# Moving w2 and the last part of wo behind the last value head, two sums behind two value heads, and the result's turn to VectorE

## The chip, the cores and the metric

The kernel runs on one core of one Trainium2 chip. The metric is the device time of one execution in microseconds. The kernel before takes 200.01 us, the median of three runs (199.66 to 200.16).

## What is computed

One decoding step of a gated mix of two branches. Branch A is attention of a single token over a cache of 4,096 positions with 32 heads of 128, followed by an output projection. Branch B is a small MLP with a squared ReLU. The gate is one scalar.

```python
x = A_x                                                     # 1 x 1 x 512
g = sigmoid((x * gate_w).sum(-1))
q = (x @ wq)                                                # 512 -> 32 heads x 128
p = softmax(einsum("bhqd,bhkd->bhqk", q, k) * 128**-0.5)    # 4096 positions
a = einsum("bhqk,bhkd->bhqd", p, v).reshape(1, 1, 4096) @ wo    # 4096 -> 512
h = relu(x @ w1 + b1)                                       # 512 -> 1376
b = (h * h) @ w2 + b2                                       # 1376 -> 512
return g * a + (1 - g) * b
```

All inputs and the result are bf16. Each key head and each value head is 1,024 KB, so 64 loads of that size are most of what is moved; wq and wo are 4,096 KB each, w1 and w2 1,376 KB each.

## The kernel before, in words

**Staging.** Eight key slots (`Kt`) and eight value slots (`Vt`), each 128 x 4,096 bf16, are refilled as their heads are used up. The SP queue issues nearly all loads in one written-out order: wq, seven key heads, then for every `h` the value head `h` and the key head `h + LAG` with `LAG = 7`. `load_k` waits until VectorE (`s_sd`) and TensorE (`s_t`) are through with the slot's former head, `load_v` until the PV product of the slot's former head (`s_pv`). Between these loads SP issues the four parts of w1 at `h == 8`, the first eight column groups of w2 (`w2a[:, 0:8, :]`, 1,024 KB) at `h == 10`, and five strips of wo at `h` 20 to 24. The other strips of wo's first 23 heads go over GpSimd's queue into `W`, where wq had been. Behind value head 31 SP issues four small or mid-sized pieces into key slots and w2 tiles: `wox` (the rows of wo for head 23, 128 KB), `w2b` (the last 96 rows of w2, 96 KB), `w2a[:, 8:10, :]` (256 KB) and `wob_sb` (the rows of wo for heads 24 to 31) in two parts of 768 and 256 KB.

**Scores.** Of each key head, VectorE multiplies and sums half of the blocks (`ttr`, L635), and TensorE turns the other half (`transposes`, L432), which ScalarE copies out and TensorE multiplies by the query (`scores`, L443). VectorE joins the halves (`smax`, L641). A maximum over four heads is made through `max_rows`, `gmax` and `max_cols`, and ScalarE takes the exponentials.

**The main loop** counts `i` from 0 to 38 on every engine. On TensorE, round `i` turns key head `i`, scores head `i - 1` and makes the PV product of head `i - 7` (`pv`, L468: 32 matmuls with one column each). MLP work is put in at `i == 24` (`mlp_h`) and `i == 27` (`mlp_out(0)`: 32 matmuls with `w2a[:, 0:8, :]`, L553). From `i == 34` on, `out_a` multiplies the parts of the projection that TensorE does for the first 23 heads' spread result (L512), while VectorE sums the other nine column groups by itself (`part_y`, L682 and L685, into `yD`). `sum_y(0)` and `sum_y(1)` (L544, four fp32 matmuls each in the trace) add that sum over the partitions into the accumulator `acc`; in rounds 36 and 37 they stand ahead of `pv(29)` and `pv(30)`. All partial results of the output, of both branches, go into `acc` in PSUM.

**The tail**, behind `pv(31)`: `norm(3)` on VectorE (L662), then `regroup` on TensorE: a transpose (L518), four matmuls with `wox` (L521), four with `w2b`, and, after VectorE's copy `oB` (L718), 16 matmuls that spread the eight heads (L526). Then `mlp_out(2)` (eight matmuls with `w2a[:, 8:10, :]`), VectorE's copy `o2B` (L720), and `out_b` (32 matmuls with `wob_sb`, L535). VectorE adds the bias (`fin`, L723), TensorE turns the 128 x 4 result to 4 x 128 (L598), VectorE copies it out of PSUM (`fin4`, L725), and SP stores it as four pieces of 256 B (L298).

[...] The functions that the change touches, and what calls them:

Of the kernel before, what the change touches and what calls it, by code (L numbers as in the profile page):

```python
# [5 lines left out]
def bass_gated_mix__gqa_block_cached__dense_activation_squared_relu__decode_kernel(  # L6
# [22 lines left out]
    bf16 = mybir.dt.bfloat16  # L29
    ALU = mybir.AluOpType  # L30
# [23 lines left out]
    NA = 24  # L54
    TB = 8
    GS = [0, 8, 10]
    TS = [0, 6, 8]
    TD = 23
    INNER, OUTER, SEAM, WRAP = range(4)
    RUNS = [(INNER, 4, 12, 0, 2), (INNER, 4, 12, 1, 2),  # L60
# [43 lines left out]
    with ctx:  # L104
        def sb(name, shape, dt):
            return ctx.enter_context(nc.sbuf_tensor(name, shape, dt))
# [28 lines left out]
        oB = sb("oB", [NH - NA, 128], bf16)  # L135
        o2A = sb("o2A", [128, 32], bf16)
        o2B = sb("o2B", [128, TB], bf16)
        fin4 = sb("fin4", [4, 128], bf16)
        zeros = sb("zeros", [128, 128], bf16)
        xb = sb("xb", [128, 4, 128], bf16)  # L140
        dm = xb[:, :, :].rearrange("p t (n a c) -> p (t n) a c", a=2, c=16)
# [18 lines left out]
        hr = sb("hr", [128, FG + 1], fp32)  # L160
        hs = sb("hs", [128, FG + 1], bf16)
        b2g = sb("b2g", [128, 4], fp32)
        fin = sb("fin", [128, 4], bf16)

        KP = [pb(f"KP{i}", [128, HB * 128], bf16) for i in range(3)]
        pS = pb("pS", [128, 512], fp32)
# [30 lines left out]
        s_wq = [sem(f"s_wq{t}") for t in range(4)]  # L197
        s_w1 = sem("s_w1")
        s_w2 = [sem(f"s_w2{n}") for n in range(len(GS))]
        s_wo = [sem(f"s_wo{n}") for n in range(len(TS) - 1)]  # L200
        s_wp = [sem(f"s_wp{n}") for n in range(len(RUNS))]
        s_dm = [sem(f"s_dm{n}") for n in range(len(RUNS))]
        s_at = sem("s_at")
# [3 lines left out]
        s_oT = sem("s_oT")  # L207
        s_oc = sem("s_oc")
        s_o2 = sem("s_o2")
        s_fT = sem("s_fT")  # L210
        s_f4 = sem("s_f4")
        s_k = [sem(f"s_k{i}") for i in range(NK)]
        s_v = [sem(f"s_v{i}") for i in range(NV)]
# [39 lines left out]
        @block.sync  # L253
        def _(eng):
            for t in range(4):
                eng.dma_start(wq_sb[:, t, :], wq_v[:, t, :]).then_inc(s_wq[t], 16)  # L256

            def load_k(h):
                if h >= NK:
                    eng.wait_ge(s_sd, h - NK + 1)  # L260
                    eng.wait_ge(s_t, 2 * (h - NK + 1))
                eng.dma_start(Kt[:, h % NK, :], k_h[h, :, :]).then_inc(s_k[h % NK], 16)

            def load_v(h):
                if h >= NV:
                    eng.wait_ge(s_pv, h - NV + 1)
                eng.dma_start(Vt[:, h % NV, :], v_h[h, :, :]).then_inc(s_v[h % NV], 16)

            for h in range(LAG):
                load_k(h)  # L270
            for h in range(NH):
                load_v(h)
                if h + LAG < NH:
                    load_k(h + LAG)
                if h == HF:
                    eng.wait_ge(s_qps, 8)
                if HF <= h < HF + len(FIRST):
                    p, st, k, q = STRIPS[len(RUNS) + h - HF]
                    eng.dma_start(W[p:p + st * (k - 1) + 1:st, :], woa_v[q:q + k, :],
                                  max_dma_last_dim=8192).then_inc(s_wr, 16)  # L280
                if h == 8:
                    eng.wait_ge(s_z, 1)
                    eng.wait_ge(s_b2, 1)
                    for t in range(4):
                        eng.dma_start(w1_sb[:, t, :], w1_v[:, t, :]).then_inc(s_w1, 16)
                if h == 10:
                    eng.dma_start(w2a[:, 0:GS[1], :], w2_v[:, 0:GS[1], :]).then_inc(s_w2[0], 16)
            eng.wait_ge(s_sd, NA + 2)
            eng.wait_ge(s_t, 2 * (NA + 2))
            eng.dma_start(wox, A_wo[HX * 128:NA * 128, :]).then_inc(s_wx, 16)  # L290
            eng.dma_start(w2b[:, :], B_w2[FG * 128:F, :]).then_inc(s_w2[1], 16)
            eng.dma_start(w2a[:, GS[1]:FG, :], w2_v[:, GS[1]:FG, :]).then_inc(s_w2[2], 16)
            for c in range(len(TS) - 1):
                eng.dma_start(wob_sb[:, TS[c]:TS[c + 1], :],
                              wob_v[:, TS[c] * DM:TS[c + 1] * DM].rearrange("p (t n) -> p t n", n=DM))\
                   .then_inc(s_wo[c], 16)
            eng.wait_ge(s_f4, 1)
            eng.dma_start(out[0, 0, :].rearrange("(j p) -> j p", p=128), fin4[:, :]).then_inc(s_out, 16)  # L298
            eng.wait_ge(s_out, 16)


# [90 lines left out]
        def _(eng):  # L392
# [111 lines left out]
            def out_a(n):  # L504
                if n == 0:
                    eng.wait_ge(s_ac, 2)
                    for q in s_wp:
                        eng.wait_ge(q, 16)
                    eng.wait_ge(s_wr, 16 * len(FIRST))
                for t in range(4 * n, min(4 * n + 4, TD)):  # L510
                    for j in range(4):
                        eng.matmul(acc[:, j:j + 1], wo_sb[:, t, j * 128:(j + 1) * 128],  # L512
                                   o2A[:, t:t + 1], start=False, stop=False,
                                   skip_group_check=True)

            def regroup():
                eng.wait_ge(s_on, NH // HPO)
                eng.transpose(KP[0][0:NH - NA, 0:128], onorm[:, NA:NH], ident[:, :]).then_inc(s_oT, 1)  # L518
                eng.wait_ge(s_wx, 16)
                for j in range(4):  # L520
                    eng.matmul(acc[:, j:j + 1], wox[:, j * 128:(j + 1) * 128], onorm[:, HX:HX + 1],  # L521
                               start=False, stop=False, skip_group_check=True)
                mlp_out(1)
                eng.wait_ge(s_oc, 1)
                for c in range(16):
                    mm = eng.matmul(O2B, selB[:, c // 8, c % 8, :], oB[:, TB * c:TB * c + TB],  # L526
                                    start=(c == 0), stop=(c == 15))
                mm.then_inc(s_oT, 1)

            def out_b(c):  # L530
                eng.wait_ge(s_o2, 1)
                eng.wait_ge(s_wo[c], 16)
                for t in range(TS[c], TS[c + 1]):
                    for j in range(4):
                        mm = eng.matmul(acc[:, j:j + 1], wob_sb[:, t, j * 128:(j + 1) * 128],  # L535
                                        o2B[:, t:t + 1], start=False, stop=(t == TB - 1),
                                        skip_group_check=True)
                if c == len(TS) - 2:
                    mm.then_inc(s_acc, 1)

            def sum_y(c):
                eng.wait_ge(s_y, 32 - TD)
# [4 lines left out]
            def mlp_out(c):  # L547
                eng.wait_ge(s_w2[c], 16)
                for n in [range(GS[1]), [FG], range(GS[1], FG)][c]:
                    M = 128 if n < FG else FR  # L550
                    w = w2a[:, n, :] if n < FG else w2b[:, :]
                    for j in range(4):
                        eng.matmul(acc[:, j:j + 1], w[:, j * 128:(j + 1) * 128], hs[0:M, n:n + 1],  # L553
                                   start=(n == 0 and j == 0), stop=False, skip_group_check=True)

            q_rows(0)
            q_cols(0)
# [3 lines left out]
            for i in range(NH + LAG):  # L561
                if i < NH:
                    transposes(i)
                if 1 <= i <= NH:
                    scores(i - 1)
                if i % 3 == 0 and i // 3 + 1 < 8:
                    q_rows(i // 3 + 1)
                if i % 3 == 2 and i // 3 + 1 < 8:
                    q_cols(i // 3 + 1)
                if i >= 5 and (i - 5) % 4 == 0 and (i - 5) // 4 < NG:  # L570
                    max_rows((i - 5) // 4)
                if i >= 6 and (i - 6) % 4 == 0 and (i - 6) // 4 < NG:
                    max_cols((i - 6) // 4)
                if i == 34:
                    out_a(0)
                if 34 <= i < 39:
                    out_a(i - 33)
                if 36 <= i < 38:
                    sum_y(i - 36)
                if i >= LAG:  # L580
                    pv(i - LAG)
                if i >= 12 and (i - 12) % HPO == 0:
                    den((i - 12) // HPO)
                if i == 24:
                    mlp_h()
                if i == 27:
                    eng.wait_ge(s_hs, 2)
                    mlp_out(0)
                if i == 32:
                    turn_a()  # L590
                if i == 33:
                    spread_a()
            regroup()
            mlp_out(2)
            for c in range(len(TS) - 1):
                out_b(c)
            eng.wait_ge(s_fin, 1)
            eng.transpose(KP[1][0:4, 0:128], fin[:, :], ident[:, :]).then_inc(s_fT, 1)  # L598


        @block.vector
        def _(eng):
            eng.memset(zeros[:, :], 0.0).then_inc(s_dz, 1)
            eng.wait_ge(s_dz, 1)
            eng.wait_ge(s_x, 32)
            eng.tensor_tensor_reduce(grow, xrow, grow, 1.0, 0.0, ALU.mult,
# [113 lines left out]
            eng.tensor_copy(o2B[:, :], O2B).then_inc(s_o2, 1)  # L720
            eng.wait_ge(s_acc, 1)
            eng.wait_ge(s_g, 4)
            eng.tensor_tensor(fin[:, :], acc[:, 0:4], b2g[:, :], ALU.add).then_inc(s_fin, 1)  # L723
            eng.wait_ge(s_fT, 1)
            eng.tensor_copy(fin4[:, :], KP[1][0:4, 0:128]).then_inc(s_f4, 1)  # L725


# [26 lines left out]
```

## Time and profile before

| | |
|---|---|
| median of three runs | 200.01 us |
| profiled execution, its own time | 199.44 us |
| its span, first to last instruction | 197.6 us |
| busy: TensorE matmul / weight load | 67% / 60% |
| busy: VectorE / ScalarE / GpSimd | 70% / 40% / 15% |
| DMA: moved, mean rate over the span | 78.76 MB, 398 GB/s |
| the loads' queue (SP), share of 16 DMA engines | 93.1% |
| TensorE's mean granted clock | 0.589 |

Times are microseconds from the span's start unless marked ns. In a timeline row the columns are start, length, engine, line, operation, out<-in, count, and in brackets the engine's idle time before it with what ended it. "issue" there means that the engine waited for nothing that the profile shows. In a row of a DMA view the last number is the median time in us from issue to landing. PE is TensorE's matmul, PEld its weight load, DVE VectorE, ACT ScalarE, POOL GpSimd, and SPq the issuing queue of SP.

### The profile page before, as it was taken

How to read it: one execution, taken by the hardware profiler on the slowest of the kernel's cores; microseconds unless marked ns; L12 is line 12 of the kernel's file. 1: busy time of each engine (PE TensorE's matmuls, PEld its weight loads, DVE VectorE, ACT ScalarE, POOL GpSimd, SP SyncE). 2: the span in 40 equal slices, each digit the busy share in tenths (PEclk: the TensorE clock that was granted, in tenths of full speed). 3: DMA queues.
4: the chain of work that ended last, by engine and by line, in shares of the span. 5: the costliest groups of instructions: out<-in, count | busy, mean ns of one | idle time of the engine just before them, and what ended most of it. 6: DMA issues, size and time to landing. Idle time of an engine off the chain costs nothing.

```text
span 197.6 us, 6567 instructions
## 1 busy us (share of the span) xinstructions
PE 132.4 (67%) x2403; PEld 119.0 (60%) x2409; DVE 139.0 (70%) x1151; ACT 79.6 (40%) x148; POOL 30.0 (15%) x53
## 2 busy tenths in 40 slices
PE   0138856799886757816567572766999876797465
PEld 0105845678686557616457462766998776787464
DVE  0307999999998687627665774767759999968501
ACT  2105857366473436503337232633048333613000
POOL 2000000000000000000008970000079770000000
PEclk9999985555555855555558555555555555555555
DMA  6999999999999999999999999999999999999970
GB/s 226 425 426 424 421 418 424 416 421 418 413 418 419 416 422 409 419 418 424 421 419 420 411 416 410 415 406 415 410 416 416 423 418 416 421 419 419 393 270 6
DMA packets 12861, 78.76 MB, mean 398 GB/s; under 512 B 2505, under 2 KB 2731, under 8 KB 3628
## 3 DMA queue, kind: packets, MB, share of 16 engines
q1 hardware_dynamic: 11278, 75.77, 93.1%
q0 software_dynamic: 1536, 2.56, 3.5%
q8 instruction: 19, 0.31, 0.6%
q14 instruction: 14, 0.11, 0.2%
q10 hardware_dynamic: 14, 0.01, 0.0%
HBM read 78.32 MB, written 0.00 MB: 396 GB/s over the span
## 4 chain that ended last, share of the span: by engine, by line
DMA 64%; DVE 23%; PE 9%; issue 2%; SPq 1%; ACT 0%; DVEq 0%
DMA Kt<-in_A_k_cache_dram 58%; DVE Kt L635 17%; DMA W<-in_A_wq_dram 6%; DVE kT L685 3%; PE pQ L468 2%; DVE S L635 1%; PE KP L432 1%; PE pQ L410 1%; PE pX L544 1%; SPq L256 1%; PE pS L443 1%; PE pX L535 0%; PE pO L468 0%; PE pX L512 0%; DVE S L641 0%
## 5 line engine op out<-in xcount | busy, mean ns | idle before, releaser
L635 DVE CUSTOM_DVE_ANT_0 Kt<-Kt,qb 128x128 bf16<-128x128 bf16 x512 | 113.3, 290 | 26.1 <-DMA Kt<-in_A_k_cache_dram 26.0
L366 ACT ACTIVATE kT<-KP 128x1024 bf16<-128x1024 bf16 x64 | 61.9, 1021 | 72.4 <-PE KP L432 72.4
L432 PE MATMUL KP<-ident,Kt 128*128 128x128 bf16 x512 | 57.5, 302 | 36.1 <-DMA Kt<-in_A_k_cache_dram 36.1
L432 PEld LDWEIGHTS KP<-ident,Kt 128*128 128x128 bf16 x512 | 49.8, 140 | 38.6 <-DMA Kt<-in_A_k_cache_dram 37.7
L635 DVE DVE_READ_ACCUMULATOR2_ANT S<- 128x1 f32 x512 | 41.6, 81 | 0.0
L443 PEld LDWEIGHTS pS<-qcol,kT 128*128 128x128 bf16 x512 | 18.7, 108 | 9.5 <-DVE S L641 9.4
L443 PE MATMUL pS<-qcol,kT 128*128 128x1 bf16 x512 | 19.2, 167 | 7.2 <-DVE S L641 7.2
L320 POOL DMA_DIRECT2D xb<-in_B_w_dram x9 | 5.3, 593 | 102.5 <-PE pQ L410 102.5
L410 PE MATMUL pQ<-W,xb 128*128 128x512 bf16 x26 | 11.4, 576 | 7.5 <-DMA W<-in_A_wq_dram 6.2
L468 PE MATMUL pO<-E,Vt 128*128 128x1 bf16 x512 | 16.1, 165 | 0.0
L468 PEld LDWEIGHTS pO<-E,Vt 128*128 128x128 bf16 x512 | 15.4, 104 | 0.9 <-issue 0.5
L338 POOL TENSOR_SCALAR_AFFINE_SELECT w_sb<-w_sb 24x36 bf16<-24x36 bf16 (+5 forms) x19 | 11.0, 579 | 2.7
L358 ACT ACTIVATE qb<-pQ 128x512 bf16<-128x512 f32 x8 | 4.7, 592 | 13.9 <-PE pQ L410 13.9
L377 ACT ACTIVATE E<-S,nM 128x32 bf16<-128x32 f32 x32 | 9.9, 309 | 0.3
L410 PEld LDWEIGHTS pQ<-W,xb 128*128 128x128 bf16 x32 | 3.5, 126 | 10.4 <-issue 10.1
L468 PE MATMUL pQ<-E,Vt 128*128 128x1 bf16 x256 | 8.1, 165 | 1.7 <-issue 1.2
L468 PEld LDWEIGHTS pQ<-E,Vt 128*128 128x128 bf16 x256 | 7.9, 106 | 1.9 <-issue 1.8
L468 PEld LDWEIGHTS pX<-E,Vt 128*128 128x128 bf16 x256 | 7.8, 104 | 0.7 <-issue 0.6
L468 PE MATMUL pX<-E,Vt 128*128 128x1 bf16 x256 | 8.1, 165 | 0.0
L323 POOL DMA_DIRECT2D W<-in_A_wo_dram x14 | 7.9, 565 | 0.0
L641 DVE COPY S<-pS 128x16 f32<-128x16 f32 x32 | 5.4, 169 | 2.3 <-PE pS L443 2.3
L621 DVE CAST qcol<-pQ 128x4 bf16<-128x4 f32 x8 | 1.2, 153 | 8.3 <-PE pQ L418 8.3
(85 smaller groups left out, 91.5 us busy)
## 6 DMA issues: line engine op xcount, KB each, us to landing
Kt<-in_A_k_cache_dram SPq DMA_DIRECT2D x32, 1024.0 KB, 27.4
Vt<-in_A_v_cache_dram SPq DMA_DIRECT2D x32, 1024.0 KB, 27.1
W<-in_A_wq_dram SPq DMA_DIRECT2D x4, 1024.0 KB, 7.9
W<-in_A_wo_dram POOLq DMA_DIRECT2D x2, 768.0 KB, 12.8
w_sb<-in_B_w_dram SPq DMA_DIRECT2D x4, 344.0 KB, 22.9
w2a<-in_B_w_dram SPq DMA_DIRECT2D x1, 1024.0 KB, 21.5
Kt<-in_A_wo_dram SPq DMA_DIRECT2D x1, 768.0 KB, 21.3
W<-in_A_wo_dram POOLq DMA_DIRECT2D x10, 64.0 KB, 23.3
```

What stands on the lines that cost most here:

```text
L320: eng.dma_start(dm[0:d, sent, :, 0:8], src[:, :, 0:8]).then_inc(s_dm[sent], 16)
L323: eng.dma_start(W[p:p + st * (k - 1) + 1:st, :], woa_v[q:q + k, :], max_dma_last_dim=8192).then_inc(s_wp[n], 16)
L338: eng.affine_select(out=part, in_=part, compare_op=ALU.not_equal, fill=1.0, base=-st * q, pattern=[[st, 4], [-1, st * (k - 1) + 1]], chann ...
L366: eng.activation(kT[:, h % 2, j * HB * 128:(j + 1) * HB * 128], KP[n % 3][:, :], ACT.Copy).then_inc(s_ev, 1)
L377: eng.activation(E[:, h % NE, :], S[:, h % NS, :], ACT.Exp, bias=nM[:, h:h + 1], scale=SCALE, accum_out=RS[:, h:h + 1]).then_inc(s_e, 1)
L410: mm = eng.matmul(pQ[:, :], xb[:, t, :], wq_sb[:, t, c * 512:(c + 1) * 512], start=(t == 0), stop=(t == 3))
L432: mm = eng.transpose(KP[n % 3][:, y * 128:(y + 1) * 128], Kt[:, h % NK, b * 128:(b + 1) * 128], ident[:, :])
L443: mm = eng.matmul(S2[:, y:y + 1], kT[:, h % 2, y * 128:(y + 1) * 128], qcol[:, h:h + 1], start=True, stop=True)
L468: mm = eng.matmul(O(h, h + 1), Vt[:, h % NV, b * 128:(b + 1) * 128], E[:, h % NE, b:b + 1], start=(b == 0), stop=(b == NB - 1))
L635: ins = eng.tensor_tensor_reduce(kb, kb, qb[:, h * 128:(h + 1) * 128], 1.0, 0.0, ALU.mult, ALU.add, S[:, h % NS, b:b + 1])
L641: eng.tensor_copy(S[:, h % NS, XB:NB], S2).then_inc(s_cp, 1)
L685: eng.scalar_tensor_tensor(out=yD, in0=wo_sb[:, t, :], scalar=o2D[:, t - TD:t - TD + 1], in1=yD, op0=ALU.mult, op1=ALU.add).then_inc(s_y, 1)
```

## The change

- `w2a[:, 0:8, :]` is no longer issued at `h == 10`; it stands behind value head 31. The order there is now `wob_sb` as one transfer of 1,024 KB, `w2a[:, 0:8, :]`, `wox`, `w2b`, `w2a[:, 8:10, :]`.
- On TensorE all of `mlp_out` moves to the very end, and the matmuls with `wox` leave `regroup`: behind `regroup` come `out_b`, `mlp_out(0)`, `out_x`, `mlp_out(1)`, `mlp_out(2)`. The accumulation's start flag goes to the first matmul of `out_a`, its stop flag and the semaphore `s_acc` to `mlp_out(2)`.
- In rounds 36 and 37 `pv` now stands ahead of `sum_y`.
- The result is turned on VectorE: `fin` becomes 128 x 4 x 32, cleared at the start, and the result goes into column 0 of each block of 32; a block transpose of 128 x 128 (in 32 x 32 blocks) brings it into rows 0, 32, 64 and 96 of `finT`. The TensorE transpose and the copy out of PSUM are gone. SP stores 16 pieces of 64 B.

```diff
# sync
-                if h == 10:
-                    eng.dma_start(w2a[:, 0:GS[1], :], w2_v[:, 0:GS[1], :]).then_inc(s_w2[0], 16)
             eng.wait_ge(s_sd, NA + 2)
             eng.wait_ge(s_t, 2 * (NA + 2))
+            eng.dma_start(wob_sb[:, :, :], wob_v.rearrange("p (t n) -> p t n", n=DM)).then_inc(s_wo, 16)
+            eng.dma_start(w2a[:, 0:GS[1], :], w2_v[:, 0:GS[1], :]).then_inc(s_w2[0], 16)
             eng.dma_start(wox, A_wo[HX * 128:NA * 128, :]).then_inc(s_wx, 16)
             eng.dma_start(w2b[:, :], B_w2[FG * 128:F, :]).then_inc(s_w2[1], 16)
             eng.dma_start(w2a[:, GS[1]:FG, :], w2_v[:, GS[1]:FG, :]).then_inc(s_w2[2], 16)
-            for c in range(len(TS) - 1):
-                eng.dma_start(wob_sb[:, TS[c]:TS[c + 1], :], ...).then_inc(s_wo[c], 16)
             eng.wait_ge(s_f4, 1)
-            eng.dma_start(out[0, 0, :].rearrange("(j p) -> j p", p=128), fin4[:, :]).then_inc(s_out, 16)
+            eng.dma_start(out[0, 0, :].rearrange("(j k a) -> k j a", j=4, k=4),
+                          finT[0:97:32, :].rearrange("k (j a) -> k j a", j=4)).then_inc(s_out, 16)
# tensor
-                if 36 <= i < 38:
-                    sum_y(i - 36)
                 if i >= LAG:
                     pv(i - LAG)
+                if 36 <= i < 38:
+                    sum_y(i - 36)
...
-                if i == 27:
-                    eng.wait_ge(s_hs, 2)
-                    mlp_out(0)
...
             regroup()
+            out_b()
+            eng.wait_ge(s_hs, 2)
+            mlp_out(0)
+            out_x()
+            mlp_out(1)
             mlp_out(2)
-            for c in range(len(TS) - 1):
-                out_b(c)
-            eng.wait_ge(s_fin, 1)
-            eng.transpose(KP[1][0:4, 0:128], fin[:, :], ident[:, :]).then_inc(s_fT, 1)
# vector
             eng.memset(zeros[:, :], 0.0).then_inc(s_dz, 1)
+            eng.memset(fin[:, :, :], 0.0).then_inc(s_fin, 1)
...
-            eng.tensor_tensor(fin[:, :], acc[:, 0:4], b2g[:, :], ALU.add).then_inc(s_fin, 1)
-            eng.wait_ge(s_fT, 1)
-            eng.tensor_copy(fin4[:, :], KP[1][0:4, 0:128]).then_inc(s_f4, 1)
+            eng.tensor_tensor(fin[:, :, 0], acc[:, 0:4], b2g[:, :], ALU.add).then_inc(s_fin, 1)
+            eng.wait_ge(s_fin, 2)
+            eng.transpose(finT[:, :], fin[:, :, :].rearrange("p j a -> p (j a)")).then_inc(s_f4, 1)
```

More of the change, by code (lines that the diff above doesn't have):

```diff
@@ L56, in bass_gated_mix__gqa_block_cached__dense_activation_squared_relu__decode_kernel @@
     GS = [0, 8, 10]
-    TS = [0, 6, 8]
     TD = 23
@@ L137, in bass_gated_mix__gqa_block_cached__dense_activation_squared_relu__decode_kernel @@
         o2B = sb("o2B", [128, TB], bf16)
-        fin4 = sb("fin4", [4, 128], bf16)
+        finT = sb("finT", [128, 128], bf16)
         zeros = sb("zeros", [128, 128], bf16)
@@ L162, in bass_gated_mix__gqa_block_cached__dense_activation_squared_relu__decode_kernel @@
         b2g = sb("b2g", [128, 4], fp32)
-        fin = sb("fin", [128, 4], bf16)
+        fin = sb("fin", [128, 4, 32], bf16)
         KP = [pb(f"KP{i}", [128, HB * 128], bf16) for i in range(3)]
@@ L199, in bass_gated_mix__gqa_block_cached__dense_activation_squared_relu__decode_kernel @@
         s_w2 = [sem(f"s_w2{n}") for n in range(len(GS))]
-        s_wo = [sem(f"s_wo{n}") for n in range(len(TS) - 1)]
+        s_wo = sem("s_wo")
         s_wp = [sem(f"s_wp{n}") for n in range(len(RUNS))]
@@ L209, in bass_gated_mix__gqa_block_cached__dense_activation_squared_relu__decode_kernel @@
         s_o2 = sem("s_o2")
-        s_fT = sem("s_fT")
         s_f4 = sem("s_f4")
@@ L292, in _ @@
             eng.dma_start(w2a[:, GS[1]:FG, :], w2_v[:, GS[1]:FG, :]).then_inc(s_w2[2], 16)
-            for c in range(len(TS) - 1):
-                eng.dma_start(wob_sb[:, TS[c]:TS[c + 1], :],
-                              wob_v[:, TS[c] * DM:TS[c + 1] * DM].rearrange("p (t n) -> p t n", n=DM))\
-                   .then_inc(s_wo[c], 16)
             eng.wait_ge(s_f4, 1)
-            eng.dma_start(out[0, 0, :].rearrange("(j p) -> j p", p=128), fin4[:, :]).then_inc(s_out, 16)
+            eng.dma_start(out[0, 0, :].rearrange("(j k a) -> k j a", j=4, k=4),
+                          finT[0:97:32, :].rearrange("k (j a) -> k j a", j=4)).then_inc(s_out, 16)
             eng.wait_ge(s_out, 16)
@@ L512, in out_a @@
                         eng.matmul(acc[:, j:j + 1], wo_sb[:, t, j * 128:(j + 1) * 128],
-                                   o2A[:, t:t + 1], start=False, stop=False,
+                                   o2A[:, t:t + 1], start=(t == 0 and j == 0), stop=False,
                                    skip_group_check=True)
@@ L518, in regroup @@
                 eng.transpose(KP[0][0:NH - NA, 0:128], onorm[:, NA:NH], ident[:, :]).then_inc(s_oT, 1)
[L519 to L523, printed above, removed]
                 eng.wait_ge(s_oc, 1)
@@ L528, in regroup, with out_b, out_x @@
                 mm.then_inc(s_oT, 1)
-            def out_b(c):
+            def out_b():
                 eng.wait_ge(s_o2, 1)
-                eng.wait_ge(s_wo[c], 16)
-                for t in range(TS[c], TS[c + 1]):
+                eng.wait_ge(s_wo, 16)
+                for t in range(TB):
                     for j in range(4):
[L535 to L539, printed above, removed]
+                        eng.matmul(acc[:, j:j + 1], wob_sb[:, t, j * 128:(j + 1) * 128], o2B[:, t:t + 1],
+                                   start=False, stop=False, skip_group_check=True)
+            def out_x():
+                eng.wait_ge(s_wx, 16)
+                for j in range(4):
+                    eng.matmul(acc[:, j:j + 1], wox[:, j * 128:(j + 1) * 128], onorm[:, HX:HX + 1],
+                               start=False, stop=False, skip_group_check=True)
             def sum_y(c):
@@ L552, in mlp_out @@
                     for j in range(4):
-                        eng.matmul(acc[:, j:j + 1], w[:, j * 128:(j + 1) * 128], hs[0:M, n:n + 1],
-                                   start=(n == 0 and j == 0), stop=False, skip_group_check=True)
+                        mm = eng.matmul(acc[:, j:j + 1], w[:, j * 128:(j + 1) * 128], hs[0:M, n:n + 1],
+                                        start=False, stop=(n == FG - 1), skip_group_check=True)
+                if c == 2:
+                    mm.then_inc(s_acc, 1)
             q_rows(0)
@@ L577, in _ @@
                     out_a(i - 33)
+                if i >= LAG:
+                    pv(i - LAG)
                 if 36 <= i < 38:
                     sum_y(i - 36)
-                if i >= LAG:
-                    pv(i - LAG)
                 if i >= 12 and (i - 12) % HPO == 0:
```

## The prediction

> **What bounds the kernel now.** I read the granted clock and the stages first (the windows view), then the loads' issue and landing times, then the last 20 us instruction by instruction.
>
> ```profile
> core 0: us, PE busy (x) PEld busy (x) DVE busy (x) ACT busy (x) POOL busy (x), PEclk, DMA share, GB/s
> 140.00:180.00 40.00, 33.75 (x674) 32.01 (x674) 34.43 (x258) 17.86 (x41) 15.65 (x21) 0.50 1.01 418
> 186.00:190.00 4.00, 4.00 (x99) 4.00 (x99) 0.21 (x1) 0.00 (x0) 0.00 (x0) 0.50 1.04 362
> 191.00:192.00 1.00, 0.00 (x0) 0.00 (x0) 0.00 (x0) 0.00 (x0) 0.00 (x0) 0.50 0.45 178
> 192.00:193.00 1.00, 0.40 (x4) 0.24 (x4) 0.23 (x1) 0.00 (x0) 0.00 (x0) 0.50 0.16 59
> 194.00:197.60 3.60, 1.53 (x41) 1.22 (x41) 0.54 (x3) 0.00 (x0) 0.00 (x0) 0.50 0.00 0
> ```
>
> The DMA engines are full (share 1.01 to 1.04) until 190 us and then run dry; the clock is 0.50 throughout this end, so it explains nothing. TensorE and VectorE follow the loads: over the span VectorE alone waited 26.0 us for key heads.
>
> ```profile
> DVE Kt L635 <- DMA Kt<-in_A_k_cache_dram: 26.0, 14, 5.4
> ```
>
> Until 190 us, then, bytes in the queue decide, and afterwards a chain of small steps. When the last loads land follows from each issue row and the landing figure under it (start plus that figure):
>
> ```profile
> 164.24 0.33 SPq L267 DMA_DIRECT2D Vt<-in_A_v_cache_dram  x1
> Vt<-in_A_v_cache_dram SPq DMA_DIRECT2D x1, 1024.0 KB, 22.6
> 169.59 0.33 SPq L267 DMA_DIRECT2D Vt<-in_A_v_cache_dram  x1
> Vt<-in_A_v_cache_dram SPq DMA_DIRECT2D x1, 1024.0 KB, 20.0
> 170.91 0.46 SPq L292 DMA_DIRECT2D w2a<-in_B_w_dram  x1
> w2a<-in_B_w_dram SPq DMA_DIRECT2D x1, 256.0 KB, 20.0
> 173.60 2.14 SPq L294 DMA_DIRECT2D Kt<-in_A_wo_dram  x1
> Kt<-in_A_wo_dram SPq DMA_DIRECT2D x1, 256.0 KB, 19.8
> ```
>
> Value head 30 lands at 186.8, head 31 at 189.6, the second part of w2 at 190.9 (with it 480 KB in 1.3 us behind head 31), the last part of wo at 193.4. So the 1,504 KB behind head 31 take 3.8 us. The end by instruction:
>
> ```profile
> 178.60 0.86 PE L512 MATMUL pX<-o2A,W 128*128 128x1 bf16 x27 [0.45 <-issue]
> 179.14 6.26 DVE L685 SCALAR_TENSOR_TENSOR kT<-W,S,kT 128x512 f32<-128x512 bf16 x8
> 185.46 1.01 PE L544 MATMUL pX<-onesf,kT 128*128 128x1 f32 x4 [2.87 <-DVE kT L685]
> 186.33 0.99 PE L468 MATMUL pQ<-E,Vt 128*128 128x1 bf16 x32
> 187.18 0.57 PE L474 MATMUL pM<-RS,onesf 128*128 128x8 f32 x2
> 190.06 0.91 PE L468 MATMUL pQ<-E,Vt 128*128 128x1 bf16 x29
> 192.21 0.24 PE L468 MATMUL pQ<-E,Vt 128*128 128x1 bf16 x3 [1.24 <-issue]
> 192.55 0.23 DVE L662 SCALAR_TENSOR_TENSOR onorm<-pQ,gcol,rden 128x8 bf16<-128x8 f32 x1 [4.55 <-PE pQ L468]
> 193.92 0.37 PE L553 MATMUL pX<-hs,w2a 128*128 128x1 bf16 x8
> 194.25 1.02 PE L535 MATMUL pX<-o2B,Kt 128*128 128x1 bf16 x32
> 195.30 0.16 DVE L723 TENSOR_TENSOR fin<-pX,b2g 128x4 bf16<-128x4 f32 x1 [1.11 <-PE pX L535]
> 195.52 0.27 PE L598 MATMUL KP<-ident,fin 128*4 128x128 bf16 x1 [0.26 <-DVE fin L723]
> 195.83 0.21 DVE L725 COPY fin<-KP 4x128 bf16<-4x128 bf16 x1 [0.36 <-PE KP L598]
> 196.06 0.29 SPq L298 DMA_DIRECT2D out_dram<-fin  x1
> ```
>
> TensorE reaches the last value head at 190.06, 0.4 us after its landing; 29 of 32 matmuls in, it stands still for 1.24 us with nothing to wait for but its own code. From the product's end (192.45) a chain of 2.8 us leads over norm, transpose, spread and `out_b` to 195.27, and only then is `acc` ready. The DMA engines have nothing left to do meanwhile. Of the 4.2 us from 193.4 to the end, none waits for a load.
>
> **The change, part by part.** *w2 behind the last head.* 1,024 KB leave the middle of the queue. At 418 GB/s that is 2.5 us, by which all later key and value heads land sooner: the queue is full, so a load lands when the bytes ahead of it are through, whatever the moment of its issue. Head 31: 189.6 - 2.5 = 187.1; head 30: 184.3. The total of bytes is unchanged, so the last landing stays about where it is: 187.1 + 3.8 + 2.5 = 193.4. The order within is new: `wob_sb` (1,024 KB) at about 189.6, `w2a[:, 0:8]` 480 KB ahead of the end, that is 193.4 - 1.3 = 192.1, the second part of w2 last. Wo's last part loses 128 packets by going in one piece; against that, small packets now stand at the very end. I take 193.4, with these bounds: were the 362 GB/s of 186 to 190 us raised to the middle's 418, the 3.8 us would be 0.5 shorter; did all 2,528 KB behind head 31 go at 362, they would take 7.2 us instead of 6.3, 0.9 longer. SP's other work is not held up: its new issues stand behind head 31's, in front of nothing but the store, some 20 us ahead of their use.
>
> *The sums behind the products.* VectorE's eight steps end at 185.40, and TensorE stood 2.87 us at L544 with `pv(29)` queued behind it. Shifted by 2.5 us they end at 182.9. In the new order `pv(29)` no longer waits; queued behind the wait are now the denominators (L474), for which VectorE's reciprocal and so `norm(3)` wait, `out_a(4)`, `pv(30)` and the second sum. From the first sum's start (185.46) to that of `pv(31)` (190.06) took 4.60 us; without `pv(29)` (186.33 to 187.18, 0.85) it is 3.75. So TensorE is free at 182.95 + 3.75 = 186.7. Head 30 (184.3) holds nothing up: the sum (0.87) and the denominators alone reach past it. Head 31 lands at 187.1, so `pv(31)` waits for its load, with 0.4 us of cover; 0.4 us more of VectorE's sum would be hidden.
>
> *The tail.* `pv(31)` 187.1 to 188.1. From its end to the start of `out_b` took 192.45 to 194.25, 1.8 us; the `wox` and `w2b` matmuls that leave that stretch lay in the wait for `oB`. So `out_b` runs 189.9 to 190.9 (wob landed 189.6). `mlp_out(0)` waits for w2 until 192.1; its 32 matmuls took 0.99 us in the middle of the kernel:
>
> ```profile
> 154.16 0.99 PE L553 MATMUL pX<-hs,w2a 128*128 128x1 bf16 x32
> ```
>
> Moving it out of there gains nothing, since TensorE waited for key heads in that stage. It ends at 193.1; eight matmuls with `wox` and `w2b` at 32 ns each bring 193.4; the last eight meet their landing at 193.4 and take 0.37: 193.8. Here the landing and TensorE's own queue arrive together, each within 0.1 us. `acc` is ready 1.5 us sooner than 195.27.
>
> *The turn.* From the end of `fin` (195.46) to the end of the copy (196.04) is 0.58 us now. VectorE's block transpose needs no other engine. [...] I take 0.25 plus 0.05 for the wait, saving 0.3. [...] The store goes from four pieces to 16; the SP wait for it is
>
> ```profile
> SPq L104 <- DMA out_dram<-fin: 0.9, 1, 0.9
> ```
>
> and I add 0.1 us, with bounds of -0.1 (other spread over the engines) and +0.9 (twice the wait). The clearing of `fin` at the start lies in the 4.80 us for which VectorE waits for x:
>
> ```profile
> 0.83 0.11 DVE L603 MEMSET zeros<- 128x64 uint32 x1 [0.83 <-PEq L739]
> 5.74 0.68 DVE L606 CUSTOM_DVE_ANT_0 w_sb<-w_sb 1x512 bf16<-1x512 bf16 x1 [4.80 <-DMA w_sb<-in_gate_w_dram]
> ```
>
> It is the same size as the memset of 0.11 us; without that cover it would cost those 0.11.
>
> *The code.* The stops at 178.60 and 192.21 come from code loading:
>
> ```profile
> q8 instruction: 19, 0.31, 0.6%
> q8 instruction: 1, 0.02, 70.2%
> q8 instruction: 1, 0.02, 70.8%
> ```
>
> 19 packets of 16 KB over the span; the single ones are from 182.5 to 182.6 and from 189.7 to 189.8. TensorE resumed 2.5 us after the second. Counted in matmuls, 127 lie between 178.60 and the product at 186.33, and 127 from there to the stop at 190.97: one packet holds that many. It seems to be asked for when the one before it is entered (186.3), starts 3.4 us later and is usable at 192.2, 5.9 us in all; whoever runs a packet's worth in 4.6 us stops. With 32 matmuls moved behind, the boundaries fall 32 matmuls later in the order: one about the end of the denominators (183.8 to 184.3), so the next is usable at 189.7 to 190.2, and that one begins some 15 matmuls into `out_b`, at 190.4. So no stop; a short one would lie in the 1.2 us from the end of `out_b` to w2's landing. The 65 matmuls left fit into that packet.
>
> **Sum** against the profiled execution (199.44 us, span 197.6, 1.8 around it): `acc` -1.5, turn -0.3, store +0.1, with rounding -1.6; span 196.0, time 197.8. The median of the runs lies 0.6 above the profiled one: 200.0 - 1.6 = 198.4 us.
>
> **The rivals.** *No shift (slower).* If SP's waits for free slots and not bytes set the landings, taking w2 out leaves a hole in the queue, head 31 stays at 189.6, and the new megabyte only lengthens the end. SP did wait:
>
> ```profile
> SPq L267 <- PE pO L468: 25.8, 9, 7.2
> ```
>
> Last landing 189.6 + 6.3 = 195.9, `acc` 196.3, end 198.45: 0.85 us later, 200.9 us. It loses time from a shift below 0.9 us on. Against it: landings come 20 us and more after their issue, in which 418 GB/s move eight megabytes, and the share is 1.01. Chance 0.07.
>
> *A late last landing.* If the 480 KB now at the end run at the dry end's 178 GB/s, they take 2.8 us instead of 1.3; last landing 194.9, `acc` 195.2, end 0.3 sooner: 199.7 us. The same comes about if a completion follows its last byte late. In the dry end the row below (192.5 to 193.0) holds the queue's last packets, and the landing is at 193.4: no more than 0.9 us.
>
> ```profile
> q1 hardware_dynamic: 14, 0.02, 11.9%
> ```
>
> [...] Chance 0.11.
>
> *The code stop stays in the tail.* If the boundary falls among the 48 matmuls behind w2's landing, 1.24 us come back: 199.6 us. My count would have to be wrong by some 17 matmuls. Chance 0.06.
>
> *A dear store.* At +0.9 instead of +0.1 the time is 199.2. Chance 0.06.
>
> **How the numbers follow.** My forecast has 0.70, at 198.4 with 197.6 to 199.3 of its own: 0.5 and 0.9 of the landing, 0.3 of the turn, in part against each other. Of no change the measurement can tell about 0.3%, 0.6 us. Faster by more than that (below 199.4): forecast and store, and a little of the late landing and the code stop, 0.80; within it 0.12; slower 0.08. The range, 197.4 to 199.7, takes in all but the no-shift case and the forecast's outer edge.
>
> **What would show it.** In the changed profile, head 31 should land near 187.1 and `pv(31)` start on it with TensorE waiting for the load; the last w2 load should land near 193.4; TensorE should wait before `mlp_out(0)` for w2, about 1 us, without an "issue" stop behind it; from the last matmul to the end there should be some 2.1 us instead of 2.3. A head 31 near 189.6 would refute the shift; a last landing past 194.5 the unchanged end of the loads; an "issue" gap behind `mlp_out(0)` the count of the code.

## The result and the profile after

The changed kernel takes 198.06 us (median of four runs, 197.99 to 198.19) against 199.83 us before (199.62 to 200.16): a ratio of 0.9911, 95% interval 0.9893 to 0.9928. The forecast was 198.4 us. The profiled execution after took 198.08 us, its span is 196.3 us. The one before took 199.44 us, 0.4 to 0.6 us less than its kernel's median, so a difference between rows can be smaller than the one between medians.

The windows view of the end, after (PE, PEld, DVE, ACT and POOL busy time with counts, then clock, DMA share and GB/s):

```profile
184.00:188.00 4.00, 3.95 (x100) 3.87 (x99) 0.21 (x1) 0.00 (x0) 0.00 (x0) 0.50 1.01 422
190.00:191.00 1.00, 0.62 (x24) 0.54 (x21) 0.00 (x0) 0.00 (x0) 0.00 (x0) 0.50 0.85 273
191.00:192.00 1.00, 0.32 (x12) 0.23 (x9) 0.00 (x0) 0.00 (x0) 0.00 (x0) 0.50 0.38 139
192.00:193.00 1.00, 0.86 (x33) 0.89 (x34) 0.00 (x0) 0.00 (x0) 0.00 (x0) 0.50 0.11 40
193.00:196.30 3.30, 0.57 (x21) 0.49 (x18) 0.49 (x2) 0.00 (x0) 0.00 (x0) 0.50 0.02 5
```

The loads end when they did before, near 193 us, at the same clock. What has changed is what TensorE still has to do then. The issue rows of three loads after, each with its landing row (issue to landing in us):

```profile
167.34 0.33 SPq L265 DMA_DIRECT2D Vt<-in_A_v_cache_dram  x1
Vt<-in_A_v_cache_dram SPq DMA_DIRECT2D x1, 1024.0 KB, 19.4
168.74 0.43 SPq L287 DMA_DIRECT2D w2a<-in_B_w_dram  x1
w2a<-in_B_w_dram SPq DMA_DIRECT2D x1, 1024.0 KB, 23.3
171.63 2.13 SPq L290 DMA_DIRECT2D w2a<-in_B_w_dram  x1
w2a<-in_B_w_dram SPq DMA_DIRECT2D x1, 256.0 KB, 21.5
```

Value head 31 lands at 186.7 (forecast 187.1, before 189.6), the large part of w2 at 192.0 (192.1), the last load at 193.1 (193.4). The timeline of the end, after:

```profile
183.21 1.01 PE L537 MATMUL pX<-onesf,kT 128*128 128x1 f32 x4 [0.43 <-DVE kT L679]
186.96 0.99 PE L463 MATMUL pQ<-E,Vt 128*128 128x1 bf16 x32
189.76 0.48 PE L525 MATMUL pX<-o2B,Kt 128*128 128x1 bf16 x12 [0.26 <-DVE o2B L714]
190.63 0.69 PE L525 MATMUL pX<-o2B,Kt 128*128 128x1 bf16 x20 [0.38 <-issue]
192.14 0.99 PE L546 MATMUL pX<-hs,w2a 128*128 128x1 bf16 x32 [0.82 <-DMA w2a<-in_B_w_dram]
193.20 0.37 PE L546 MATMUL pX<-hs,w2a 128*128 128x1 bf16 x8
193.61 0.17 DVE L717 TENSOR_TENSOR fin<-pX,b2g 128x4 bf16<-128x4 f32 x1 [3.90 <-PE pX L546]
193.82 0.31 DVE L719 STREAM_TRANSPOSE finT<-fin 128x128 bf16<-128x128 bf16 x1
194.16 0.65 SPq L292 DMA_DIRECT2D out_dram<-finT  x1
```

The product of head 31 is unbroken; the code stop has moved into `out_b` and is short (0.38 us); TensorE then waits 0.82 us for w2. Against before, `acc` is ready 1.70 us sooner (193.57 for 195.27), the turn takes 0.35 us from the end of `fin` instead of 0.58, and from the end of the turn (194.13) to the end of the span it takes 2.17 us instead of 1.56. The sum, -1.70 - 0.23 + 0.61 = -1.3, is the difference of the spans. The late end of the store is the one large surprise.

### The profile page after: what moved, and what is told of

Same layout as the page of the kernel before. It is cut to its first block, busy times and chain, and to the rows that moved or that the text cites. A ratio compares the mean times of both kernels' runs of the same rounds, so it can differ in the third digit from the quotient of the medians.

```text
span 196.3 us, 6564 instructions
## 1 busy us (share of the span) xinstructions
PE 132.9 (68%) x2402; PEld 118.8 (61%) x2408; DVE 139.5 (71%) x1152; ACT 79.5 (41%) x148; POOL 29.9 (15%) x53
## 4 chain that ended last, share of the span: by engine, by line
DMA 59%; DVE 22%; PE 9%; SPq 6%; issue 3%; ACT 0%
DMA Kt<-in_A_k_cache_dram 42%; DVE Kt L629 18%; DMA w2a<-in_B_w_dram 12%; DMA W<-in_A_wq_dram 6%; SPq L265 4%; PE KP L427 3%; PE pX L481 2%; DVE S L629 1%; SPq L260 1%; PE pQ L405 1%; PE pX L477 1%; PE pX L546 1%; SPq L254 1%; PE pS L438 1%; DVE dg L644 0%
## 5 line engine op out<-in xcount | busy, mean ns | idle before, releaser
L427 PE MATMUL KP<-ident,Kt 128*128 128x128 bf16 x512 | 56.8, 300 | 32.8 <-DMA Kt<-in_A_k_cache_dram 32.8
L629 DVE DVE_READ_ACCUMULATOR2_ANT S<- 128x1 f32 x512 | 41.0, 80 | 0.0
L405 PE MATMUL pQ<-W,xb 128*128 128x512 bf16 x26 | 12.4, 620 | 7.8 <-DMA W<-in_A_wq_dram 6.4
```

The source lines that it names most:

```text
L405: mm = eng.matmul(pQ[:, :], xb[:, t, :], wq_sb[:, t, c * 512:(c + 1) * 512], start=(t == 0), stop=(t == 3))
L427: mm = eng.transpose(KP[n % 3][:, y * 128:(y + 1) * 128], Kt[:, h % NK, b * 128:(b + 1) * 128], ident[:, :])
L629: ins = eng.tensor_tensor_reduce(kb, kb, qb[:, h * 128:(h + 1) * 128], 1.0, 0.0, ALU.mult, ALU.add, S[:, h % NS, b:b + 1])
```

## The experiments

In these runs the kernel before had medians between 199.84 and 200.04 us. "The changed kernel" is 198.06.

**1. Fewer bytes in the middle** (the kernel before; seven column groups of w2 are left out).

```diff
-  eng.dma_start(w2a[:, 0:GS[1], :], w2_v[:, 0:GS[1], :]).then_inc(s_w2[0], 16)   # h == 10
+  eng.dma_start(w2a[:, 0:1, :], w2_v[:, 0:1, :]).then_inc(s_w2[0], 16)
-  w = w2a[:, n, :] if n < FG else w2b[:, :]
+  w = w2a[:, 0 if c == 0 else n, :] if n < FG else w2b[:, :]
```

> The kernel before, with only the first column group of w2 loaded in the middle (128 KB instead of 1,024 KB), and used for all eight groups. Theory (all later landings follow the bytes ahead of them): 896 KB less at 418 GB/s bring every later landing and the end 2.2 us forward: value head 31 lands at 187.4, 197.8 us. Rival (free slots set the landings, a hole opens in the queue): value head 31 near 189.6, 200.0 us, with DMA share below 0.95 somewhere behind 75 us.

Measured: 197.85 us, ratio 0.9896 (0.9881 to 0.9911). Value head 31:

```profile
167.55 0.33 SPq L267 DMA_DIRECT2D Vt<-in_A_v_cache_dram  x1
Vt<-in_A_v_cache_dram SPq DMA_DIRECT2D x1, 1024.0 KB, 20.1
190.78 0.24 PE L468 MATMUL pQ<-E,Vt 128*128 128x1 bf16 x3 [1.51 <-issue]
```

It lands at 187.65 instead of 189.6, and the median falls by 2.1 us with the code stop still in the product (third row). The DMA share stays at 1.01 to 1.02 from 60 to 180 us, so the queue holds no hole; the bytes ahead set the landing.

**2. w2 back in the middle, all else as changed.**

```diff
+  if h == 10:
+      eng.dma_start(w2a[:, 0:GS[1], :], w2_v[:, 0:GS[1], :]).then_inc(s_w2[0], 16)
...
-  eng.dma_start(w2a[:, 0:GS[1], :], w2_v[:, 0:GS[1], :]).then_inc(s_w2[0], 16)    # behind wob
```

> The changed kernel, with the 1,024 KB of w2 loaded where they were before, in the middle; TensorE's order is that of the changed kernel. Theory (the bytes ahead of value head 31 set its landing): head 31 lands 2.5 us later, near 189.3; its product ends 190.5, out_b runs 192.3 to 193.3, w2's matmuls are no longer hidden and end at 194.9, span 197.6, time 199.4 us. Rival (only the code stop matters, which this order keeps away from the product): 198.1 us.

Measured: 199.55 us, ratio 0.9979 (0.9970 to 0.9988). Head 31 lands at 169.62 + 19.5 = 189.1, and w2's matmuls, though loaded long ago, stand behind the product's chain:

```profile
189.48 0.99 PE L464 MATMUL pQ<-E,Vt 128*128 128x1 bf16 x32
193.53 0.99 PE L547 MATMUL pX<-hs,w2a 128*128 128x1 bf16 x32
194.60 0.35 PE L547 MATMUL pX<-hs,w2a 128*128 128x1 bf16 x8
```

So the place of the load is worth 1.5 us of the changed kernel, given TensorE's new order.

**3. The sums ahead of the products again** (the changed kernel).

```diff
+  if 36 <= i < 38:
+      sum_y(i - 36)
   if i >= LAG:
       pv(i - LAG)
-  if 36 <= i < 38:
-      sum_y(i - 36)
```

> The changed kernel, with the sums of VectorE's rows ahead of the two value heads as before. Theory: the product of value head 31 starts at 187.5 instead of 186.9 us, out_b ends near 191.9 with the code stop, and w2 lands at 192.0, so the delay is hidden: 198.1 us. Rival (the order is what pays): 198.6 us or more.

Measured: 198.11 us, ratio 0.9907 (0.9895 to 0.9920): no difference. The product starts at 187.89, 0.9 us later than in the changed kernel, and `out_b` still ends ahead of w2's landing:

```profile
187.89 0.99 PE L463 MATMUL pQ<-E,Vt 128*128 128x1 bf16 x32
192.15 0.99 PE L546 MATMUL pX<-hs,w2a 128*128 128x1 bf16 x32 [0.45 <-DMA w2a<-in_B_w_dram]
```

**4. Only the sums moved** (the kernel before; the reverse of 3).

> The kernel before, with only the two sums put behind the value heads. Theory: TensorE is free for value head 31 before it lands at 189.6 instead of 190.06, which alone is worth 0.4 us; the code boundaries lie in the same number of matmuls, now one inside pv(29)'s end, entered near 185 us instead of 186.3, so the next packet is usable by 191 and the stop shrinks to some 0.3 us or less: 200.0 - 1.3 = 198.7 us. Rival (the stop stays as long as it was): 199.6 us.

Measured: 198.97 us, ratio 0.9955 (0.9941 to 0.9969), between the two expectations' ends and nearer to the theory.

```profile
190.01 0.91 PE L468 MATMUL pQ<-E,Vt 128*128 128x1 bf16 x29 [0.30 <-DMA Vt<-in_A_v_cache_dram]
191.64 0.24 PE L468 MATMUL pQ<-E,Vt 128*128 128x1 bf16 x3 [0.72 <-issue]
```

The product starts on its load, as expected, but hardly sooner than before (190.06), since head 31 lands at 189.9 in this profile. What these rows gain is that the stop is shorter and ends at 191.64 instead of 192.21: 0.57 us. The medians differ by 1.0 us, and no trace shows where an execution of the kernel before that is as long as its median spends the rest. So an edit that is worth nothing in the changed kernel is worth 0.6 to 1 us alone, and what the rows show of it comes by way of the code.

**5. Eight matmuls more in round 27** (the kernel before).

```diff
       mlp_out(0)
+      for _ in range(8):
+          eng.matmul(acc[:, 0:1], ident[:, :], zeros[:, 0:1], start=False, stop=False, skip_group_check=True)
```

> The kernel before, with eight more matmuls (zero added into acc) behind mlp_out(0) in round 27, where TensorE waits for key heads anyway. Theory (a code packet holds some 127 matmuls and is asked for when the one before is entered, usable 5.9 us later): the boundary that lay behind the first sum now lies ahead of it, in the wait for VectorE, so the next packet is asked for by about 182.6 and usable at 188.5, and the stop of 1.24 us in the product of value head 31 is gone: 200.0 - 1.2 = 198.8 us. Rival (the stop is no code loading, but a wait that the profile does not show, or lies in time and not in the order of the code): 200.0 us, with the stop still near 191 us.

Measured: 199.93 us, ratio 0.9997 (0.9987 to 1.0008). A miss, and a useful one:

```profile
184.39 0.25 PE L512 MATMUL pX<-o2A,W 128*128 128x1 bf16 x4 [2.11 <-issue]
192.21 0.46 PE L468 MATMUL pQ<-E,Vt 128*128 128x1 bf16 x11 [1.42 <-issue]
q8 instruction: 1, 0.02, 66.4%
```

Both boundaries now come eight matmuls sooner in the order, as the count says (the product stops behind 21 of 32). But at the first one TensorE stood still for 2.11 us, so it was entered only at 184.39, not at 182.6. The next packet (the last row, of the window from 189.7 to 189.8) began 5.3 us later and was usable at 192.21 again. So the count of matmuls held and the forecast of the time failed: the boundary was entered 1.9 us sooner than before (186.33), and the transfer of the next packet began no sooner. Why, no run here tells; that the stop is tied to a moment and not to the code is what experiment 6 tests.

**6. Thirty-two matmuls fewer** (the kernel before; the accumulation's start flag moves to the first matmul of `out_a`).

```diff
       eng.wait_ge(s_hs, 2)
-      mlp_out(0)
+      eng.wait_ge(s_w2[0], 16)
```

> The kernel before, without the 32 matmuls of mlp_out(0) in round 27 (that part of the MLP is left out; its load and wait stay). The code boundaries then fall 32 matmuls later in the order, as in the changed kernel, and nothing else moves: the stop that lay 29 matmuls into the product of value head 31 would come 28 matmuls behind that product, ahead of the last parts of the tail. Theory (a code boundary with its packet usable near 192.2 us makes the stop, and only its place in the order costs): the product of head 31 runs through from 190.06 to 191.05, the boundary is reached near 192.6 with the code there, and the kernel is 1.2 us faster than before: 198.8 us. Rival (the time of TensorE's stop is fixed, wherever the boundary lies, as the kernel with eight more matmuls might be read): a stop until 192.2 stays and the time is 200.0 us.

Measured: 198.71 us, ratio 0.9934 (0.9920 to 0.9948), as the theory has it.

```profile
190.09 0.99 PE L468 MATMUL pQ<-E,Vt 128*128 128x1 bf16 x32
193.18 0.27 PE L553 MATMUL pX<-hs,w2a 128*128 128x1 bf16 x4 [0.36 <-issue]
```

Head 31 lands when it did (189.6), the product begins when it did and runs through the moment at which it stood still before, and 1.3 us of the median are gone (1.0 us of `acc` in the profiles, 194.30 for 195.27), because the boundary now lies behind it. A stop of 0.36 us remains further on, in the middle of `mlp_out(2)`.

**7. The turn and the store as before** (the changed kernel): `fin` 128 x 4, TensorE's transpose, the copy `fin4`, four pieces of 256 B.

> The changed kernel, but the result is turned by TensorE and copied out of PSUM as before, and stored in four pieces of 256 B. Theory: VectorE's turn saved 0.23 us (0.58 to 0.35 from the end of fin) and the store of 16 pieces lost 0.61 us (from the end of the turn to the end of the span 1.56 before, 2.17 after), so this kernel is 0.4 us faster than the changed one: 197.7 us. Rival (the longer store is a chance of that one profile): 0.2 us slower than the changed one, 198.3 us.

Measured: 197.82 us (197.66 to 197.84), ratio 0.9891 (0.9878 to 0.9904): faster than the changed kernel, whose own runs lie at 197.99 to 198.19, by 0.24 us where 0.4 were expected. The two ratios' intervals overlap, but so small a difference has a second witness: experiment 3's kernel, with the changed turn and store and run in the same rounds, took 197.99 to 198.23.

```profile
194.21 0.21 DVE L720 COPY fin<-KP 4x128 bf16<-4x128 bf16 x1 [0.36 <-PE KP L593]
194.45 0.29 SPq L293 DMA_DIRECT2D out_dram<-fin  x1
```

From the copy's end (194.42) to the span's end (196.0) are 1.6 us again. VectorE's turn, as stored, costs more than it saves.

**8. VectorE's turn with four pieces of 256 B.** The output columns are dealt to `acc` in steps of four, so that the transpose's output can be written in the result's order.

```diff
-  wob_sb[:, t, j * 128:(j + 1) * 128]            # and so for wo_sb, wox, yD and w2
+  wob_sb[:, t, j::4]
-  eng.transpose(finT[:, :], fin[:, :, :].rearrange("p j a -> p (j a)"))
+  eng.transpose(finT[:, :].rearrange("p (a j) -> p j a", j=4), fin[:, :, :])
-  eng.dma_start(out[0, 0, :].rearrange("(j k a) -> k j a", j=4, k=4), ...)
+  eng.dma_start(out[0, 0, :].rearrange("(k n) -> k n", k=4), finT[0:97:32, :])
```

> The changed kernel, with the 512 output columns dealt to the four accumulator columns in steps of four, so that VectorE's block transpose can write each of the four rows in the order of the output and the store is four pieces of 256 B again. b2 is loaded once more as a 128 x 4 tile. Theory: the number of pieces is what made the store long, so it takes 1.56 us from the turn and the kernel 198.1 - 0.6 = 197.5 us. Rival (the store is long because VectorE's transpose is reported done late): 198.1 us. If weight loads with a step of four elements are slower than dense ones (104 ns each), the tail shows it in the 44 weight loads behind w2's landing.

Measured: 198.67 us, ratio 0.9938 (0.9926 to 0.9950). Slower than the changed kernel; both expectations fail on the total.

```profile
190.56 1.14 PEld L526 LDWEIGHTS pX<-o2B,Kt 128*128 128x128 bf16 x32 [0.34 <-DVE o2B L715]
192.56 1.20 PE L547 MATMUL pX<-hs,w2a 128*128 128x1 bf16 x32 [0.77 <-DMA w2a<-in_B_w_dram]
194.54 0.46 DVE L720 STREAM_TRANSPOSE finT<-fin 128x128 bf16<-128x128 bf16 x1
195.03 0.61 SPq L293 DMA_DIRECT2D out_dram<-finT  x1
```

With four pieces the issue is still 0.61 us and the end of the span still 2.1 us behind the turn (195.00 to 197.1): the number of pieces was not the cause. Of the 0.8 us by which this span exceeds the changed kernel's, about half is the step's own: from the start of w2's matmuls to `acc` takes 1.74 us instead of 1.43, and the transpose 0.46 us instead of 0.31. (In `out_b`, 32 weight loads take 1.14 us, where the kernel of experiment 7 takes 0.95.) The other half is that w2 lands later in this profile, so that its matmuls start at 192.56 instead of 192.14; whether that belongs to the edit is not shown.

**9. TensorE's turn, but spread over rows 0, 32, 64 and 96.** The kernel of experiment 7, with the store's source laid out as in the change.

```diff
-  eng.transpose(KP[1][0:4, 0:128], fin[:, :], ident[:, :])
+  eng.transpose(KP[1][:, 0:128], fin[:, :, :].rearrange("p j a -> p (j a)"), ident[:, :])
-  eng.tensor_copy(fin4[:, :], KP[1][0:4, 0:128])
+  eng.tensor_copy(finT[:, :], KP[1][:, 0:128])
-  eng.dma_start(out[0, 0, :].rearrange("(j p) -> j p", p=128), fin4[:, :])
+  eng.dma_start(out[0, 0, :].rearrange("(j p) -> j p", p=128), finT[0:97:32, :])
```

> The changed kernel with the turn on TensorE, but spread: fin is 128 x 4 x 32 and cleared as in the change, TensorE turns all 128 columns, VectorE copies 128 x 128 out of PSUM, and the store takes rows 0, 32, 64 and 96 as four pieces of 256 B. Theory (the step of 32 partitions in the store's source is what makes its issue 0.6 us long): issue near 0.6 us, 2.1 us from the end of the copy to the end of the span, time 197.8 + 0.6 = 198.4 us. Rival (VectorE's transpose is what delays the store): issue 0.29 us, 1.6 us to the end, 197.9 us.

Measured: 198.34 us, ratio 0.9917 (0.9903 to 0.9930), as the theory has it.

```profile
194.29 0.22 DVE L721 COPY finT<-KP 128x128 bf16<-128x128 bf16 x1 [0.38 <-PE KP L593]
194.54 0.61 SPq L293 DMA_DIRECT2D out_dram<-finT  x1
```

No VectorE transpose, four pieces, and the same long store: 0.61 us to issue, 2.1 us to the end (196.6). Against experiment 7 it is the store's source that differs on this path, so what costs is the step of 32 partitions. Why such a source is slower than four adjacent partitions, no run here tells.

**10. w2 in three parts, each used when it lands** (the kernel of experiment 7).

```diff
-  GS = [0, 8, 10]
+  GS = [0, 4, 8, 10]                 # load order: wob, wox, w2b, then the three parts; matmuls in the same order
```

> The changed kernel with the turn on TensorE, and behind value head 31 the order wob, wox, w2b, then w2 in groups 0 to 3, 4 to 7, 8 and 9, each multiplied when it lands. Theory (the last landing near 193.1 us sets the end, and TensorE's 32 matmuls behind one 1,024 KB landing cost a little on top): TensorE has only eight matmuls left behind the last landing, acc near 193.5 instead of 193.65, 197.7 us. Rival (the last landing moves with the sizes of the last loads): 197.3 us if it comes sooner with larger packets at the end, 198.2 us if later.

Measured: 198.00 us, ratio 0.9901 (0.9887 to 0.9915). No gain: 0.2 us slower than experiment 7, between the theory and the rival's later landing.

```profile
w2a<-in_B_w_dram SPq DMA_DIRECT2D x1, 256.0 KB, 19.7
192.87 1.00 PE L546 MATMUL pX<-hs,w2a 128*128 128x1 bf16 x24 [0.66 <-DMA w2a<-in_B_w_dram]
```

The last 256 KB, now issued at 173.7, land at 193.4, where experiment 7's kernel has 193.2. TensorE has only eight matmuls left then, but it ends them at 193.87, not at 193.66. Whether the smaller loads put the landing back, one profile of each does not show.

**11. The code boundaries back at their old places** (the kernel of experiment 7).

```diff
+  if i == 27:
+      for _ in range(32):
+          eng.matmul(acc[:, 0:1], ident[:, :], zeros[:, 0:1], start=True, stop=True, skip_group_check=True)
```

> The changed kernel with the turn on TensorE (197.82 us), and 32 more matmuls (of zeros, overwritten later) in round 27, where mlp_out(0) stood before: the code boundaries fall back to the places that they had in the kernel before, the last one 29 matmuls into the product of value head 31. Theory (the new order of the loads leaves over a microsecond between out_b and w2's landing, which takes in such a stop): a stop of about 1.3 us in the product, its end near 189.7, out_b 191.5 to 192.5, then w2's matmuls 0.3 us later than without the stop: 198.1 us. Rival (the gain of the change is all in the boundary's place): 197.8 + 1.3 = 199.1 us.

Measured: 197.92 us, ratio 0.9903 (0.9886 to 0.9919).

```profile
188.78 0.22 PE L463 MATMUL pQ<-E,Vt 128*128 128x1 bf16 x3 [0.85 <-issue]
190.81 1.01 PE L525 MATMUL pX<-o2B,Kt 128*128 128x1 bf16 x32 [0.26 <-DVE o2B L719]
192.27 0.99 PE L546 MATMUL pX<-hs,w2a 128*128 128x1 bf16 x32 [0.44 <-DMA w2a<-in_B_w_dram]
```

The stop is back, 29 matmuls into the product, as in the kernel before, and costs next to nothing: the wait for w2 behind it shrinks from 1.09 us in experiment 7 to 0.44, and `acc` is ready at 193.68 instead of 193.66. The gain of the change is therefore not a lucky boundary.

## Why the prediction was right, point by point

**Bytes decide the landings: right.** Head 31 came 2.85 us sooner (forecast 2.5), and the last landing stayed, 0.3 us early. Experiments 1 and 2 show it from both sides; "no shift" is refuted. In the seven kernels here that load w2 behind head 31 (the changed one and experiments 3 and 7 to 11), head 31 lands between 186.7 and 187.1, so some tenths of the 2.85 are scatter between profiles.

**The late last landing did not come.** Of the queue's packets the last ones after lie between 192.5 and 193.0, the row of that window being

```profile
q1 hardware_dynamic: 4, 0.00, 2.3%
```

and the landing is at 193.13, at most 0.6 us after them. A completion that follows its last byte by more than these 0.6 us did not appear on SP's queue here.

**The sums: right in the term, needless in the total.** TensorE was free at 186.96 (forecast 186.7), so the product started there and not on its load (186.74); instead of a cover of 0.4 us, TensorE came 0.2 us behind the landing. Experiment 3 shows that 0.9 us more is hidden too.

**The tail: right.** `acc` at 193.57 against 193.8.

**The code: the count held, the time did not.** A stop was forecast away and came, behind 12 matmuls of `out_b` instead of none near the 15th, 0.38 us long, and hidden in the wait that the prediction named as its cover. The boundary before it was entered at 184.08, as forecast, but its successor's code was usable only 6.5 us later, at 190.63, where the prediction had 5.9 us. That estimate is no constant: it was 7.8 in experiment 5. Only its second half, from the packet to the code's use, is steady (2.4 to 2.6 us in the three profiles), and that a packet is asked for when the one before it is entered is shown by no run.

**Where the time came from.** The prediction priced the end by the new last landing, and that sum holds. It did not say how much of it undoes the code stop alone. Experiment 6 takes the stop out of the product without moving a load and gains 1.3 us; experiment 7, loads moved and the old turn, gains 2.2 us against the same runs of before (197.82 to 199.99); experiment 11 keeps 1.9 us with the stop left in. So the two routes overlap: either takes the stop off the path, and moving the loads gains only about 0.9 us beyond that.

**The turn and the store: wrong.** The turn saved 0.23 us (forecast 0.3). The 0.25 us that the forecast took for VectorE's transpose were the author's estimate, and no run shows them: the transpose took 0.31 us, where VectorE's copy of the same 128 x 128 in experiment 9 took 0.22. The store was the step that failed: +0.61 us where the sum had +0.1. It lay within the stated bound of +0.9, but the reason given, more pieces, was not the cause (experiments 8 and 9). The wait on SP's semaphore, the row on which the price rested, grew little:

```profile
SPq L103 <- DMA out_dram<-finT: 1.1, 1, 1.1
```

The larger part is in the issue itself, 0.65 us for 0.29, a row that the prediction quoted and did not price. The early `acc` makes up for part of this late store: in spans the forecast was -1.6 and the result -1.3. (The forecast's own terms, -1.47, -0.3 and +0.1, come to -1.67.) That the medians nevertheless differ by 1.8 is because the profiled execution before lies under its kernel's median (199.44 against 199.83 to 200.01), while the one after lies at its own (198.08 against 198.06). The prediction had added that difference to the kernel after as well. So between profiles the gain fell 0.3 us short of the forecast, and the median came out 0.3 us better than forecast: that 198.4 came so near to 198.06 is in part luck.

## What to carry to other kernels

Where the loads' queue is full to the end (here a DMA share of 1.00 to 1.02 from 60 to 188 us), put what is used last also last in the queue (here value head 31 landed 2.85 us sooner), and count what each engine still has to do behind the last landing; a wait left in front of that landing is cover in which stops and delays vanish (here 0.9 us of delay in experiment 3 cost nothing, and a stop of 0.85 us in experiment 11 cost 0.1). Before an order is credited with a gain, look for an "issue" stop on the path: adding or removing some matmuls far away moved it here (eight in experiment 5, 32 in experiments 6 and 11), and told whether the order or the code's boundary paid. Price a store by its issue row too, and by how its source's partitions lie, not by its bytes alone (here 0.29 us or 0.61 to 0.65, for the same 1.0 KB).

## What was not expected of the hardware

- In the kernel before and in the changed one the queue q8, marked "instruction", moved 19 packets, 0.31 MB in all, so 16 KB each. Between two of TensorE's "issue" stops lie 127 matmuls with their weight loads in experiment 5 (184.39 to 192.21) and in experiment 11 (182.53 to 188.78), and twice as many in the kernel before (178.60 to 192.21) and in the changed kernel (177.05 to 190.63); 19 packets of 127 make about the 2,403 matmuls that the profile counts. TensorE went on 2.4 to 2.6 us after the packet in the kernel before, in experiment 5 and in the changed kernel, where the packet is in the window from 188.0 to 188.1,

```profile
q8 instruction: 1, 0.02, 63.9%
```

  and TensorE resumes at 190.62. By that count of 127, the time from entering one packet to the start of the next packet's transfer was 3.4 us before, 4.0 us in the changed kernel and 5.3 us in experiment 5. The stop in the product before came among dense one-column matmuls, which used up a packet in 4.6 us (186.33 to 190.97).
- A store whose source has a step of 32 partitions took 0.61 to 0.65 us to issue instead of 0.29, and 0.5 to 0.6 us longer to the end of the span, with 16 pieces (the changed kernel) or with four (experiments 8 and 9).
- Weight loads with a step of four bf16 elements took 1.14 us for 32 (experiment 8), against 0.95 us dense (experiment 7).
